# Moving work at both ends of a fused S5 + Mish-MLP kernel: a sum in the tail, two transposes and one layernorm in the head

## The chip, the cores and the metric

The kernel runs on one core of one Trainium2 chip. The metric is the device time of one execution in microseconds (us). Every execution quoted here is of the undisturbed ("fast") state, with a granted TensorE clock of 0.999 or 1.0. Engines are named as in the profile: PE (TensorE matmul), PEld (its weight loads), DVE (VectorE), ACT (ScalarE), POOL (GpSimd), SP (SyncE, here only a DMA queue).

## The reference, cut to what matters

```python
def reference(A_x, Lambda.., B.., C.., log_dt, Dskip, B_x, w1, b1, w2):   # S = 2048, D = 1024, F = 3584
    x  = A_x
    xn = _layernorm(x)
    # _A_ref: Bu = xn @ B_bar.T; h_t = Lam_bar * h_(t-1) + Bu_t; y = 2 Re(h @ C.T) + xn * Dskip
    # _B_ref: h = xn @ w1 + b1; act = h * tanh(softplus(h)); act @ w2
    return x + _A_ref(xn, ...) + _B_ref(xn, w1, b1, w2)
```

The 2048 tokens are worked in four blocks of 512. A block consists of: the 28 weight tiles of `w1` (PE, each evicted by DVE), the projection of the state inputs (PE, evicted by DVE into `mt`), the recurrence as scans (DVE), and the output sums of `w2` and `C` over eight units, one PSUM bank each (PE).

## The kernel before

The head of the program. Layernorm of the first four token tiles, transposes on PE, and small filler matmuls that keep PE busy while its clock rises:

```python
    keep_busy(44)                       # filler matmuls, 128x128
    ... transpose of the parameters
    keep_busy(12)
    for q in range(2):                  # tiles 0 and 1: statistics on DVE, root on ACT
        first_sums_v(q, 0); first_sums_v(q, 1); first_var_v(q); first_sqrt(q)
    first_apply(0)                      # DVE: xn of tile 0
    first_transpose(0)                  # PE: eight 128x128 transposes
    keep_busy(4)
    first_apply(1)
    first_transpose(1)
    keep_busy(4)
    first_copy(0, VE, 0, 4); first_copy(1, VE, 0, 4)      # PSUM -> xnT
    first_copy(0, AC, 4, NK); first_copy(1, AC, 4, NK)
    first_mean_a(3)                     # tile 3: sums on ACT, behind ACT's copies
    ... tile 2's statistics on DVE, tile 3's on ACT
    first_apply(2); first_apply(3)
    NSPLIT = 6
    for f in range(NSPLIT):             # first six weight tiles on tokens 0..255 only
        first_half(f, 0)                # eight 128x256 matmuls
        if f in (2, 4):
            q = 1 + f // 2              # tile 2 behind the third, tile 3 behind the fifth weight tile
            first_transpose(q)
            first_copy(q, VE)
```

Then small DVE operations give `thp`, and POOL starts its phases from it: eight times three operations (`px`, `py`, `ph`), 128x512 f32 in SBUF, with the loads of block 1's `x` issued by POOL in between:

```python
    def phases(j):
        pop(tensor_scalar(px, iot, thp[j], mult)); pop(tensor_scalar(py, px, +magic, -magic)); pop(tensor_tensor(xs, px, py, subtract))
    for j in range(NJ):
        phases(j)
        if j == 3:
            for q in range(NQ): load_x(PO, 1, q)
```

The tail of the last block:

```python
        for q in range(NQ):
            units = (2 * q, 2 * q + 1) if not (ends and q == NQ - 1) else (2 * q,)
            ... proj(j, ci, u, ...) for the last NJ - njt .. NJ
            finish(q, 0, len(units) * TB)                            # DVE: xx += ps, then store from ACT
        if ends:
            tmp, b_tmp = ct[0]
            vop(tensor_tensor(tmp, ps[:, 7, :], xx[:, i, 3, TB:D], add))      # first sum of unit 7
            for h in range(2):
                ... proj_quarter(...)                                # six 128x256 matmuls
                vop(tensor_tensor(xx[...], ps[:, h, 0:256], tmp[...], add))
                out_events["end", h] = AC.dma(...)                   # both stores issued by ACT
```

Of the kernel before, what the change touches and what calls it, by code (L numbers as in the profile page):

```python
# [5 lines left out]
ALU = mybir.AluOpType  # L6
# [150 lines left out]
def build_kernel(nc, A_x, A_Lambda_re, A_Lambda_im, A_B_re, A_B_im, A_C_re, A_C_im,  # L157
                 A_log_dt, A_Dskip, B_w1, B_b1, B_w2, out):
    bf16, f32, i32 = DT.bfloat16, DT.float32, DT.int32
    S, D = A_x.shape[1], A_x.shape[2]  # L160
    NP = A_Lambda_re.shape[0]
    F = B_w1.shape[1]
    TB = 512
    NB = S // TB
    NQ = TB // P
    NK = D // P
# [9 lines left out]
    VE = Queue(nc, "ve")  # L176
    AC = Queue(nc, "ac")
    PO = Queue(nc, "po")
    SP = Queue(nc, "sp")

    def sb(name, shape, dtype):
# [26 lines left out]
    xx = sb("xx", [P, 2, NQ, D], bf16)  # L208
    b_xx = [[Buf("xx%d_%d" % (i, q), parts=[Buf("xx%d_%d_%d" % (i, q, h)) for h in range(2)])
             for q in range(NQ)] for i in range(2)]  # L210
    s_xx = [[DmaSem(nc, "d_xx%d_%d" % (i, q)) for q in range(NQ)] for i in range(2)]
    xn = sb("xn", [P, NQ, D], bf16)
    b_xn = [Buf("xn%d" % q) for q in range(NQ)]
    mt = sb("mt", [P, 2, 2, TB], bf16)
    b_m = [Buf("m%d" % i) for i in range(2)]
    dsk = sb("dsk", [P, D], bf16)
# [5 lines left out]
    b_ident = Buf("ident")  # L222
# [142 lines left out]
        aop(lambda e: e.activation(rc(q, 1), mv[:, q, 1:2], AF.Sqrt, scale=scale, bias=kon[:, 2:3]),  # L365
            reads=[b_mv[q], b_kon], writes=[b_rs1[q]])

    def first_apply(q):
        y = rc(q, 1)
        vop(lambda e: e.reciprocal(y, y), reads=[b_rs1[q]], writes=[b_rs1[q]])  # L370
        vop(lambda e: e.tensor_scalar(xn[:, q, :], xx[:, 0, q, :], mv[:, q, 0:1], y,
                                      op0=ALU.subtract if q < 3 else ALU.add, op1=ALU.mult),
            reads=[b_xx[0][q], b_mv[q], b_rs1[q]], writes=[b_xn[q]])

    def bank_T(q, k):
        if q < 2 and k >= NK // 2:
# [3 lines left out]
    def first_transpose(q):  # L380
        for k in range(NK):
            bank = bank_T(q, k)
            PE.mm(lambda e, k=k, bank=bank: e.transpose(ps16(bank)[:, k * P:(k + 1) * P],  # L383
                                                        xn[:, q, k * P:(k + 1) * P], ident[:]),
                  reads=[b_xn[q], b_ident], writes=[b_ps[bank]],
                  first=k == 0 or bank != bank_T(q, k - 1), last=k == NK - 1 or bank != bank_T(q, k + 1))

    def first_copy(q, queue, k0=0, k1=NK):
        dst = xnT[:, k0:k1, q * P:(q + 1) * P]
        bank = bank_T(q, k0)  # L390
        srcp = ps16(bank).rearrange("p (k t) -> p k t", k=NK)[:, k0:k1, :]
        b_dst = b_xnT[q] if k1 - k0 == NK else b_xnT[q].parts[k0 // 4]
        if queue is AC:
            aop(lambda e: e.copy(dst, srcp), reads=[b_ps[bank]], writes=[b_dst])
        else:
            vop(lambda e: e.tensor_copy(dst, srcp), reads=[b_ps[bank]], writes=[b_dst])  # L396
# [63 lines left out]
    def keep_busy(n):  # L460
        for i in range(n):
            PE.mm(lambda e: e.matmul(ps[:, 3, 0:P], lhsT=ident[:], rhs=ident[:], start=True, stop=True),  # L462
                  reads=[b_ident], writes=[b_ps[3]], first=i == 0, last=i == n - 1)

    keep_busy(44)
    aop(lambda e: e.activation(rs[:, :, 3], kon[:, 2:3].to_broadcast([P, NQ]), AF.Sqrt), reads=[b_kon], writes=b_rs)
    PE.op(lambda e: e.transpose(ps16(2)[:, 0:NST], st[:, :], ident[0:NST, 0:NST]),  # L467
          reads=[b_st, b_ident], writes=[b_ps[2]])
# [5 lines left out]
        first_sqrt(q)  # L474
    first_apply(0)
    first_transpose(0)
    keep_busy(4)
    first_apply(1)
    first_transpose(1)
    keep_busy(4)  # L480
    first_copy(0, VE, 0, 4)
    first_copy(1, VE, 0, 4)
    first_copy(0, AC, 4, NK)
# [8 lines left out]
    first_sqrt(3)  # L492
    first_apply(2)
    first_apply(3)
    NSPLIT = 6

    def first_half(f, half):
        s, fi = f // 2, f % 2
        wt = ring[:, s, :].rearrange("p (k f) -> p k f", k=NK)
        ts = slice(half * 256, half * 256 + 256)  # L500
        for k in range(NK):
            PE.mm(lambda e, k=k: e.matmul(ps[:, f, ts], lhsT=wt[:, k, fi * P:(fi + 1) * P], rhs=xnT[:, k, ts],  # L502
                                          start=k == 0, stop=k == NK - 1),
                  reads=[b_ring[s]] + [b.parts[k // 4] for b in b_xnT[2 * half:2 * half + 2]], writes=[b_ps[f]],
                  first=half == 0 and k == 0, last=half == 1 and k == NK - 1)

    for f in range(NSPLIT):
        first_half(f, 0)
        if f in (2, 4):
            q = 1 + f // 2  # L510
            first_transpose(q)
            first_copy(q, VE)

    aop(lambda e: e.activation(c("dt"), ldt, AF.Exp), reads=[b_par], writes=[b_cs["dt"]])
    small("a", "dt", lre, ALU.mult)
# [198 lines left out]
    out_events = {}  # L714
    b_end = [Buf("end%d" % h) for h in range(2)]
    def tail(blk):
        first = [True] * 8

        def acc(u, lhsT, rhs, reads, last=False):
            st_ = first[u]  # L720
            first[u] = False
            PE.mm(lambda e: e.matmul(ps[:, u, :], lhsT=lhsT, rhs=rhs, start=st_, stop=last),  # L722
                  reads=reads, writes=[b_ps[u]], first=st_, last=last)

        def dense(f, s, units):
            wt = ring[:, s, :].rearrange("p (f d) -> p f d", f=2)
            for u in units:
                q, h = u // 2, u % 2
                acc(u, act[:, f, q * P:(q + 1) * P], wt[:, f % 2, h * TB:(h + 1) * TB], [b_actf[f], b_ring[s]])

        def proj(j, ci, u, last):
            q, h = u // 2, u % 2
            acc(u, hT[:, ci, j, q * P:(q + 1) * P], CT[:, ci, j, h * TB:(h + 1) * TB], [b_hT[ci][j], b_CT[j]], last)

        def proj_quarter(j, ci, bank, lo, st_, last):
            PE.mm(lambda e: e.matmul(ps[:, bank, 0:256], lhsT=hT[:, ci, j, 3 * P:4 * P], rhs=CT[:, ci, j, lo:lo + 256],
                                     start=st_, stop=last),
                  reads=[b_hT[ci][j], b_CT[j]], writes=[b_ps[bank]], first=st_, last=last)

        njt = 1 if blk == 0 else 3  # L740
        base = n_item[0]
        for f in range(6):
            dense(f, (base + f // 2) % NRING, (4, 5, 6, 7))
        for f in range(NF):
            dense(f, (base + f // 2) % NRING, (0, 1, 2, 3) if f < 6 else range(8))
            if f % 2 == 1:
                item_done()
            if blk + 1 < NB and f in (7, 9, 11, 13):
                transpose_dma((f - 7) // 2)
        for j in range(NJ - njt):  # L750
            for ci in range(2):
                for u in range(8):
                    proj(j, ci, u, blk == NB - 1 and u == 7 and j == NJ - njt - 1 and ci == 1)
        i = blk % 2

        def store(q, lo, hi, sem):
            r0 = blk * TB + q * P
            b_x = b_xx[i][q] if hi - lo > TB else b_xx[i][q].parts[lo // TB]
            out_events[i, q, lo] = AC.dma(lambda e: e.dma_start(out[0, r0:r0 + P, lo:hi], xx[:, i, q, lo:hi]),
                                          sem, reads=[b_x])  # L760

        def finish(q, lo, hi):
            bank, n = 2 * q + lo // TB, (hi - lo) // TB
            b_x = b_xx[i][q] if n > 1 else b_xx[i][q].parts[lo // TB]
            xr = xx[:, i, q, lo:hi]
            src = ps[:, bank:bank + n, :].rearrange("p a t -> p (a t)")
            vop(lambda e: e.tensor_tensor(xr, src, xr, op=ALU.add), reads=b_ps[bank:bank + n] + [b_x], writes=[b_x])  # L767
            store(q, lo, hi, s_out[i][q])

        ends = blk == NB - 1  # L770
        for q in range(NQ):
            units = (2 * q, 2 * q + 1) if not (ends and q == NQ - 1) else (2 * q,)
            for j in range(NJ - njt, NJ):
                for ci in range(2):
                    for u in units:
                        proj(j, ci, u, j == NJ - 1 and ci == 1)
            finish(q, 0, len(units) * TB)
        if ends:

            tmp, b_tmp = ct[0]  # L780
            b_x = b_xx[i][3].parts[1]
            vop(lambda e: e.tensor_tensor(tmp[:], ps[:, 7, :], xx[:, i, 3, TB:D], op=ALU.add),  # L782
                reads=[b_ps[7], b_x], writes=[b_tmp])
            for h in range(2):
                lo = TB + 256 * h
                for j in range(NJ - njt, NJ):
                    for ci in range(2):
                        proj_quarter(j, ci, h, lo, j == NJ - njt and ci == 0, j == NJ - 1 and ci == 1)
                vop(lambda e, h=h, lo=lo: e.tensor_tensor(  # L789
                    xx[:, i, 3, lo:lo + 256], ps[:, h, 0:256], tmp[:, 256 * h:256 * h + 256], op=ALU.add),  # L790
                    reads=[b_ps[h], b_tmp], writes=[b_end[h]])
                r0 = blk * TB + 3 * P
                out_events["end", h] = AC.dma(lambda e, lo=lo, r0=r0: e.dma_start(
                    out[0, r0:r0 + P, lo:lo + 256], xx[:, i, 3, lo:lo + 256]), DmaSem(nc, "d_end%d" % h), reads=[b_end[h]])
        if blk + 2 < NB:
            for q in range(NQ):
                load_x(PO, blk + 2, q)
# [81 lines left out]
```

## Time and profile before

The three runs before the prediction took 622.5, 623.05 and 625.32 us. The profiled execution took 621.96 us and spans 620.5.

| stretch of the profiled run | us | what it is |
|---|---|---|
| 0 to 8.69 | 8.7 | loads, layernorm of two tiles, fillers, transposes |
| 8.69 to 20.25 | 11.6 | six split weight tiles, transposes of tiles 2 and 3 |
| 20.25 to 616.56 | 596.3 | PE without a pause |
| 616.56 to 620.5 | 3.9 | last sums and stores |

The chain of waits of the kernel before, followed back from the last instruction (start in us, length in us, engine, tile, line):

```profile
8.69 2.78 PE ps L502 x24
...
14.21 6.20 PE ps L502 x56
20.41 37.99 PE ps L644 x176
58.40 27.63 PE ps L664 x128
86.03 75.97 PE ps L722 x352
...
616.58 0.69 DVE xx L767
617.27 0.61 DVE ct L782
...
617.98 0.76 DVE xx L789 x2
```

PE carries it nearly alone. L502 are the split tiles, L644 the full weight tiles, L664 the projection, L722 the output sums.

Two more lines of the same profile follow. The first is the table of busy times of 28 to 91 us (the columns are stretch, length, and busy us with instruction counts of PE, PEld, DVE, ACT and POOL, then clock, DMA share and GB/s):

```profile
28.00:91.00 63.00, 63.00 (x293) 28.58 (x292) 60.52 (x101) 59.02 (x44) 31.62 (x21) 1.00 1.05 232
```

The second is the only wait of PE or PEld between 20 and 110 us (engine, tile, line, whom it waited for: us in total, times, longest):

```profile
PEld ps L722 <- DVE mt L669: 0.3, 1, 0.3
```

A weight load waited for an `mt` eviction of DVE, at 91.46 us.

The tail in the timeline (start, length, engine, line; "q" is an engine's DMA issue):

```profile
615.29 1.99 DVE L767 TENSOR_TENSOR xx<-ps,xx 128x1024 bf16<-128x1024 f32 x2 [1.36 <-PE ps L722]
...
617.19 0.68 DVE L782 TENSOR_TENSOR ct<-ps,xx 128x512 f32<-128x512 f32 x1
617.98 0.76 DVE L789 TENSOR_TENSOR xx<-ps,ct 128x256 bf16<-128x256 f32 x2
618.43 0.82 ACTq L793 DMA_DIRECT2D out_dram<-xx  x2
```

PE's last matmul ends at 617.85. Behind it stand a sum that could have been made long before (L782), two quarter sums, and two stores issued one after the other.

### The profile page before, as it was taken

How to read it: one execution, taken by the hardware profiler on the slowest of the kernel's cores; microseconds unless marked ns; L12 is line 12 of the kernel's file. 1: busy time of each engine (PE TensorE's matmuls, PEld its weight loads, DVE VectorE, ACT ScalarE, POOL GpSimd, SP SyncE). 2: the span in 40 equal slices, each digit the busy share in tenths (PEclk: the TensorE clock that was granted, in tenths of full speed). 3: DMA queues.
4: the chain of work that ended last, by engine and by line, in shares of the span. 5: the costliest groups of instructions: out<-in, count | busy, mean ns of one | idle time of the engine just before them, and what ended most of it. 6: DMA issues, size and time to landing. Idle time of an engine off the chain costs nothing.

```text
span 620.5 us, 7405 instructions
## 1 busy us (share of the span) xinstructions
PE 616.3 (99%) x2967; PEld 288.1 (46%) x2967; DVE 466.3 (75%) x689; ACT 244.8 (39%) x158; POOL 49.9 (8%) x47
## 2 busy tenths in 40 slices
PE   8999999999999999999999999999999999999998
PEld 8544444444444444444444444444444444444443
DVE  6899999999467599998147659999624856999603
ACT  5679995440079940000009992000001999000000
POOL 1998000000100000000010000000000000000000
PEclk9999999999999999999999999999999999999999
DMA  9999967740464301773065420285204541033001
GB/s 262 239 274 270 223 142 205 202 136 0 161 178 141 132 1 40 217 185 103 17 191 165 140 99 1 98 209 167 70 35 137 168 137 67 1 135 104 1 0 69
DMA packets 124476, 79.41 MB, mean 128 GB/s; under 512 B 48922, under 2 KB 106906, under 8 KB 124442
## 3 DMA queue, kind: packets, MB, share of 16 engines
q1 hardware_dynamic: 120800, 71.58, 42.6%
q10 hardware_dynamic: 2682, 4.21, 1.9%
q0 software_dynamic: 960, 3.15, 1.7%
q8 instruction: 24, 0.39, 0.3%
q14 instruction: 10, 0.08, 0.0%
HBM read 63.19 MB, written 4.19 MB: 109 GB/s over the span
## 4 chain that ended last, share of the span: by engine, by line
PE 99%; DVE 0%; POOL 0%; issue 0%; DVEq 0%; POOLq 0%
PE ps L722 49%; PE ps L644 29%; PE ps L664 18%; PE ps L502 2%; PE ps L462 1%; PE ps L383 0%; DVE xx L789 0%; DVE xx L767 0%; DVE ct L782 0%; DVE xnT L396 0%; POOL ident L330 0%; POOL ident L329 0%; DVE par L486 0%; PE ps L467 0%; POOL kon L333 0%
## 5 line engine op out<-in xcount | busy, mean ns | idle before, releaser
L722 PE MATMUL ps<-ring,act 128*128 128x512 bf16 x896 | 194.0, 379 | 0.0
L644 PE MATMUL ps<-xnT,ring 128*128 128x512 bf16 x848 | 183.7, 379 | 0.0
L622 ACT ACTIVATE act<-hb 128x3584 bf16<-128x3584 bf16 x16 | 51.0, 3185 | 244.1 <-DVE hb L651 243.8
L722 PEld LDWEIGHTS ps<-ring,act 128*128 128x128 bf16 x896 | 87.6, 98 | 105.8 <-DVE mt L669 0.3
L644 PEld LDWEIGHTS ps<-xnT,ring 128*128 128x128 bf16 x848 | 83.0, 98 | 99.9
L651 DVE TENSOR_SCALAR hb<-ps,par 128x512 bf16<-128x512 f32 x112 | 82.7, 746 | 55.1 <-PE ps L644 53.6
L664 PE MATMUL ps<-xnT,BT 128*128 128x512 bf16 x512 | 111.2, 379 | 0.0
L722 PE MATMUL ps<-CT,hT 128*128 128x512 bf16 x506 | 109.9, 379 | 0.0
L669 DVE TENSOR_TENSOR mt<-ps,tab 128x1024 bf16<-128x1024 f32 x64 | 75.4, 1219 | 13.3 <-PE ps L664 11.7
L664 PEld LDWEIGHTS ps<-xnT,BT 128*128 128x128 bf16 x512 | 50.1, 98 | 60.4
L722 PEld LDWEIGHTS ps<-CT,hT 128*128 128x128 bf16 x506 | 49.5, 98 | 59.7
L767 DVE TENSOR_TENSOR xx<-ps,xx 128x1024 bf16<-128x1024 f32 (+1 forms) x16 | 18.8, 1190 | 69.5 <-PE ps L722 69.4
L687 DVE TENSOR_TENSOR_SCAN hT<-cs,qi,hT 128x512 bf16<-128x512 f32 x48 | 58.9, 1269 | 0.0
L624 ACT ACTIVATE act<-act 128x3584 bf16<-128x3584 bf16 x16 | 51.1, 3192 | 0.2
L623 ACT ACTIVATE act<-act 128x3584 bf16<-128x3584 bf16 x16 | 51.1, 3192 | 0.2
L692 DVE TENSOR_TENSOR mt<-hT,tab 128x1024 bf16<-128x1024 bf16 x64 | 41.4, 688 | 1.1
L629 DVE TENSOR_TENSOR act<-act,hb 128x3584 bf16<-128x3584 bf16 x16 | 32.3, 2018 | 1.3 <-ACT act L624 1.3
L287 POOL DMA_DIRECT2D xx<-in_A_x_dram x12 | 6.7, 560 | 253.0 <-DVE xx L767 248.7
L598 ACT ACTIVATE ct<-CT,cs 128x512 f32<-128x512 bf16 x16 | 11.5, 720 | 28.8 <-DVE CT L600 24.5
L623 ACT ACT_TABLE_LOAD x16 | 20.5, 1283 | 0.3
L624 ACT ACT_TABLE_LOAD x16 | 20.5, 1283 | 0.3
L687 DVE TENSOR_TENSOR_SCAN hT<-cs,hT 128x512 bf16<-128x512 f32 x16 | 18.7, 1208 | 0.0
(82 smaller groups left out, 281.3 us busy)
## 6 DMA issues: line engine op xcount, KB each, us to landing
ring<-in_B_w_dram SPq DMA_DIRECT2D x112, 512.0 KB, 3.8
out_dram<-xx ACTq DMA_DIRECT2D x15, 256.0 KB, 2.1
xx<-in_A_x_dram POOLq DMA_DIRECT2D x12, 256.0 KB, 4.6
xx<-in_A_x_dram SPq DMA_DIRECT2D x3, 256.0 KB, 5.0
xx<-in_A_x_dram SPq DMA_DIRECT2D x2, 128.0 KB, 2.1
dsk<-in_A_Dskip_dram SPq DMA_DIRECT2D x1, 256.0 KB, 6.7
xnT<-xn SPq DMA_TRANSPOSE x12, 4.5
BT<-in_A_B_re_dram SPq DMA_TRANSPOSE x8, 6.0
```

The lines of the kernel that those rows point to most:

```text
L622: aop(lambda e: e.activation(a, hs, AF.Exp), reads=[b_hb[g % 2]], writes=[b_act[g]])
L623: aop(lambda e: e.activation(a, a, AF.Ln, bias=1.0), reads=[b_act[g]], writes=[b_act[g]])
L624: aop(lambda e: e.activation(a, a, AF.Tanh), reads=[b_act[g]], writes=[b_act[g]])
L629: vop(lambda e: e.tensor_tensor(a, a, hs, op=ALU.mult), reads=[b_act[g], b_hb[g % 2]], writes=[b_act[g]])
L644: PE.mm(lambda e, k=k: e.matmul(ps[:, bank, :], lhsT=wt[:, k, fi * P:(fi + 1) * P], rhs=xnT[:, k, :], start=k == 0, stop=k == NK - 1), rea ...
L651: vop(lambda e: e.tensor_scalar(hb[:, hs, :], ps[:, bank, :], b1(f), None, op0=ALU.add), reads=[b_ps[bank], b_par], writes=[b_hbf[hs]])
L664: PE.mm(lambda e, j=j, ci=ci, k=k, bank=bank: e.matmul(ps[:, bank + ci, :], lhsT=BT[:, ci, j, k, :], rhs=xnT[:, k, :], start=k == 0, stop= ...
L669: vop(lambda e, s=s, u=u, j=j: e.tensor_tensor(mt[:, s, :, :], u, tab[:, s, j, :].unsqueeze(1).to_broadcast([P, 2, TB]), op=ALU.mult), rea ...
L687: vop(lambda e, ci=ci, init=init: e.tensor_tensor_scan(out=hT[:, ci, j, :], data0=cj("r", j).to_broadcast([P, TB]), data1=hT[:, ci, j, :], ...
L692: vop(lambda e, s=s: e.tensor_tensor(mt[:, s, :, :], hT[:, :, j, :], tab[:, s, j, :].unsqueeze(1).to_broadcast([P, 2, TB]), op=ALU.mult), ...
L722: PE.mm(lambda e: e.matmul(ps[:, u, :], lhsT=lhsT, rhs=rhs, start=st_, stop=last), reads=reads, writes=[b_ps[u]], first=st_, last=last)
L767: vop(lambda e: e.tensor_tensor(xr, src, xr, op=ALU.add), reads=b_ps[bank:bank + n] + [b_x], writes=[b_x])
```

## The change

The intent in the tail: make the first sum of the last unit early, while DVE is idle, and issue the two end stores from two queues. In the head: put the transposes of tiles 2 and 3 inside and behind the fourth weight tile, so that five split tiles are enough; apply tile 1's layernorm in halves, so that its transposes can start on the first half; and move the fillers to where PE would wait.

```diff
@@ -210,7 +210,7 @@
              for q in range(NQ)] for i in range(2)]
     s_xx = [[DmaSem(nc, "d_xx%d_%d" % (i, q)) for q in range(NQ)] for i in range(2)]
     xn = sb("xn", [P, NQ, D], bf16)
-    b_xn = [Buf("xn%d" % q) for q in range(NQ)]
+    b_xn = [Buf("xn%d" % q, parts=[Buf("xn%d_%d" % (q, h)) for h in range(2)]) for q in range(NQ)]
     mt = sb("mt", [P, 2, 2, TB], bf16)
     b_m = [Buf("m%d" % i) for i in range(2)]
     dsk = sb("dsk", [P, D], bf16)
@@ -365,12 +365,15 @@
         aop(lambda e: e.activation(rc(q, 1), mv[:, q, 1:2], AF.Sqrt, scale=scale, bias=kon[:, 2:3]),
             reads=[b_mv[q], b_kon], writes=[b_rs1[q]])
 
-    def first_apply(q):
+    def first_apply(q, pieces=1):
         y = rc(q, 1)
         vop(lambda e: e.reciprocal(y, y), reads=[b_rs1[q]], writes=[b_rs1[q]])
-        vop(lambda e: e.tensor_scalar(xn[:, q, :], xx[:, 0, q, :], mv[:, q, 0:1], y,
-                                      op0=ALU.subtract if q < 3 else ALU.add, op1=ALU.mult),
-            reads=[b_xx[0][q], b_mv[q], b_rs1[q]], writes=[b_xn[q]])
+        for h in range(pieces):
+            d = slice(h * D // pieces, (h + 1) * D // pieces)
+            b_x, b_o = (b_xx[0][q], b_xn[q]) if pieces == 1 else (b_xx[0][q].parts[h], b_xn[q].parts[h])
+            vop(lambda e, d=d: e.tensor_scalar(xn[:, q, d], xx[:, 0, q, d], mv[:, q, 0:1], y,
+                                               op0=ALU.subtract if q < 3 else ALU.add, op1=ALU.mult),
+                reads=[b_x, b_mv[q], b_rs1[q]], writes=[b_o])
 
     def bank_T(q, k):
         if q < 2 and k >= NK // 2:
@@ -382,7 +385,7 @@
             bank = bank_T(q, k)
             PE.mm(lambda e, k=k, bank=bank: e.transpose(ps16(bank)[:, k * P:(k + 1) * P],
                                                         xn[:, q, k * P:(k + 1) * P], ident[:]),
-                  reads=[b_xn[q], b_ident], writes=[b_ps[bank]],
+                  reads=[b_xn[q].parts[k // (NK // 2)], b_ident], writes=[b_ps[bank]],
                   first=k == 0 or bank != bank_T(q, k - 1), last=k == NK - 1 or bank != bank_T(q, k + 1))
 
     def first_copy(q, queue, k0=0, k1=NK):
@@ -462,7 +465,7 @@
             PE.mm(lambda e: e.matmul(ps[:, 3, 0:P], lhsT=ident[:], rhs=ident[:], start=True, stop=True),
                   reads=[b_ident], writes=[b_ps[3]], first=i == 0, last=i == n - 1)
 
-    keep_busy(44)
+    keep_busy(48)
     aop(lambda e: e.activation(rs[:, :, 3], kon[:, 2:3].to_broadcast([P, NQ]), AF.Sqrt), reads=[b_kon], writes=b_rs)
     PE.op(lambda e: e.transpose(ps16(2)[:, 0:NST], st[:, :], ident[0:NST, 0:NST]),
           reads=[b_st, b_ident], writes=[b_ps[2]])
@@ -474,10 +477,9 @@
         first_sqrt(q)
     first_apply(0)
     first_transpose(0)
-    keep_busy(4)
-    first_apply(1)
+    first_apply(1, 2)
     first_transpose(1)
-    keep_busy(4)
+    keep_busy(6)
     first_copy(0, VE, 0, 4)
     first_copy(1, VE, 0, 4)
     first_copy(0, AC, 4, NK)
@@ -492,24 +494,27 @@
     first_sqrt(3)
     first_apply(2)
     first_apply(3)
-    NSPLIT = 6
-
-    def first_half(f, half):
+    NSPLIT = 5
+
+    def first_half(f, half, k0=0, k1=NK):
         s, fi = f // 2, f % 2
         wt = ring[:, s, :].rearrange("p (k f) -> p k f", k=NK)
         ts = slice(half * 256, half * 256 + 256)
-        for k in range(NK):
+        for k in range(k0, k1):
             PE.mm(lambda e, k=k: e.matmul(ps[:, f, ts], lhsT=wt[:, k, fi * P:(fi + 1) * P], rhs=xnT[:, k, ts],
                                           start=k == 0, stop=k == NK - 1),
                   reads=[b_ring[s]] + [b.parts[k // 4] for b in b_xnT[2 * half:2 * half + 2]], writes=[b_ps[f]],
                   first=half == 0 and k == 0, last=half == 1 and k == NK - 1)
 
     for f in range(NSPLIT):
-        first_half(f, 0)
-        if f in (2, 4):
-            q = 1 + f // 2
-            first_transpose(q)
-            first_copy(q, VE)
+        first_half(f, 0, 0, NK // 2)
+        if f == 3:
+            first_transpose(2)
+            first_copy(2, VE)
+        first_half(f, 0, NK // 2, NK)
+        if f == 3:
+            first_transpose(3)
+            first_copy(3, VE)
 
     aop(lambda e: e.activation(c("dt"), ldt, AF.Exp), reads=[b_par], writes=[b_cs["dt"]])
     small("a", "dt", lre, ALU.mult)
@@ -768,6 +773,11 @@
             store(q, lo, hi, s_out[i][q])
 
         ends = blk == NB - 1
+        if ends:
+            tmp, b_tmp = ct[0]
+            b_x7 = b_xx[i][3].parts[1]
+            vop(lambda e: e.tensor_tensor(tmp[:], ps[:, 7, :], xx[:, i, 3, TB:D], op=ALU.add),
+                reads=[b_ps[7], b_x7], writes=[b_tmp])
         for q in range(NQ):
             units = (2 * q, 2 * q + 1) if not (ends and q == NQ - 1) else (2 * q,)
             for j in range(NJ - njt, NJ):
@@ -777,10 +787,6 @@
             finish(q, 0, len(units) * TB)
         if ends:
 
-            tmp, b_tmp = ct[0]
-            b_x = b_xx[i][3].parts[1]
-            vop(lambda e: e.tensor_tensor(tmp[:], ps[:, 7, :], xx[:, i, 3, TB:D], op=ALU.add),
-                reads=[b_ps[7], b_x], writes=[b_tmp])
             for h in range(2):
                 lo = TB + 256 * h
                 for j in range(NJ - njt, NJ):
@@ -790,7 +796,7 @@
                     xx[:, i, 3, lo:lo + 256], ps[:, h, 0:256], tmp[:, 256 * h:256 * h + 256], op=ALU.add),
                     reads=[b_ps[h], b_tmp], writes=[b_end[h]])
                 r0 = blk * TB + 3 * P
-                out_events["end", h] = AC.dma(lambda e, lo=lo, r0=r0: e.dma_start(
+                out_events["end", h] = (SP, AC)[h].dma(lambda e, lo=lo, r0=r0: e.dma_start(
                     out[0, r0:r0 + P, lo:lo + 256], xx[:, i, 3, lo:lo + 256]), DmaSem(nc, "d_end%d" % h), reads=[b_end[h]])
         if blk + 2 < NB:
             for q in range(NQ):
```

## The prediction

> **What bounds the kernel now.** PE. On the page PE is busy 616.3 us of the 620.5 us span; in the chain of waits it holds 99%, and from 8.69 us (first real matmul) to 616.56 us it runs through four blocks with no wait. The change touches only the two ends.
>
> **Tail (timeline, 607 to 620.5).** Last PE result about 617.85. DVE before: unit 6's sum 616.58 (0.69), the first sum of unit 7 617.19 (0.68), then two quarter sums 617.98 and 618.33 (0.42 each); both stores are issued by ACT one after the other (618.43, 618.85; 0.41 each), the last lands 1.7 us later and ends the span. Bank 7's first sum is complete about 607.5, and DVE idles until 610.11, so moving it there is free. Then: first quarter sum 617.23 (when its matmuls are done), its store on SP; second quarter sum 617.88 to 618.30, store at 618.35, landing about 620.0. Saves 0.5 us, all critical.
>
> **Head (timeline, 6 to 21).** Matmul work hardly changes (128x256 matmuls start every 109 ns, 128x512 every 216: one split tile less saves 0.02 us). What counts is stalls; before there are two of 0.09 us (tile 2's transpose waits for xn at 11.40; the second token half waits for the copy of tile 3 at 14.99).
> - Four more fillers delay tile 0's transpose: it starts at 7.02, behind the twelve fillers, though its xn ended at 6.85. Estimate +0.2 us (44 fillers took 4.8 us, about 107 ns each; the twelve after 6.3 us 57 ns each). The Trainium skill ("TensorE: Matmul & The Clock Gate", Part 1) says the activity window is free-running, so this varies by run; this trace shows one such change only.
> - Removing the four fillers between the transposes gives that back to tile 1: it starts at 7.69 as before. The halves of its layernorm hide nothing then (xn ended at 7.50). First real matmul still about 8.7.
> - ACT's two copies follow tile 0's transpose, so they end 0.2 later (9.15 for 8.93), and with them tile 3's whole ACT chain (mean 1.15, square 1.13, root 0.29, then DVE 0.16 and 0.55): xn of tile 3 is ready about 13.1 for 12.88.
> - PE now asks for tile 3's transpose after four tiles and one transpose, about 8.7+0.07+3.95 = 12.7, where before it asked at 13.60 and had 0.7 us of slack. New stall about 0.45 us, plus some 0.1 for the copy of tile 3 before the second half, and 0.07 in tile 0 for the ACT copies.
>
> Head, less tile 2's stall: about +0.4 us. Nothing later absorbs it, since PE never waits later.
>
> **Sum.** +0.4 - 0.5 = about -0.1 us: no visible change. Predicted 622.8 us, 8 in 10 between 621.8 and 624.0. Faster by over 2%: 0.005; within 2%: 0.99; slower by over 2%: 0.005.
>
> **What would show it.** Right: in the timeline the first-sum DVE instruction stands near 607.6 (relative to PE's end), the last store is issued 0.5 us after PE's last matmul ends instead of 1.0; PE idles 0.3 to 0.5 us before tile 3's transposes, released by DVE's xn; tile 0's transposes start 0.2 later, tile 1's at the same time. Wrong: no idle there, or the first real matmul before 8.5.
>
> **What would make it wrong.** The clock rising at another moment (moves the head by up to 0.4); a weight slot landing later than PE asks; a slower store from SP; a faster ACT chain; or run-to-run noise larger than the effect, which I expect.

## More of the kernel before

In block 0 DVE does more than evict weight tiles. Between the evictions stand coefficients, the skip product `x += xn * dsk` (lines with `mt<-xn,dsk` and `xx<-xx,mt`), and the layernorm of block 1:

```python
            if f in (7, 8, 9, 10):      coefficients(f - 7)
            if f in (9, 11, 12, 13):    ln_skip(0, ...)
            if f in (14, 16, 18, 20):   ln_stats_only(1, (f - 14) // 2)
            if f == 22:                 ln_rsqrt()
            if f in (23, 24, 25, 26):   ln_scale(1, f - 23)
        ...
        project_in(blk)        # per j: 16 matmuls, then DVE: two 'mt<-ps,tab', two 'hT<-mt'
```

The output sums of a block begin with the four units whose banks come free first. The other four need the last `mt` evictions of the projection:

```python
        for f in range(6):
            dense(f, ..., (4, 5, 6, 7))                              # 24 matmuls
        for f in range(NF):
            dense(f, ..., (0, 1, 2, 3) if f < 6 else range(8))       # waits for mt of the last two j
```

## The result, and the profile after

The changed kernel: 623.32 us median of 6 runs (622.52 to 623.98). The kernel before in the same comparison: 622.58 (621.94 to 625.32). The ratio of the fast runs is 1.0005, 95% interval 0.9985 to 1.0024: no difference at 2%. Ratios in this text are the mean time of one kernel's fast runs over that of the other's of the same rounds, so they are not quite the ratio of the quoted medians. Here one run of 625.32 lifts the mean of before, so the means differ by only 0.3 us where the medians differ by 0.7. By both the changed kernel is the slower one, but the interval does not exclude a tie.

The profiled execution took 623.57 us and spans 622.1, which is 1.6 us more than that of before. Its chain of waits:

```profile
11.60 1.48 PE ps L504 x12
...
19.74 39.71 PE ps L649 x184
59.45 27.63 PE ps L669 x128
87.08 4.12 PE ps L727 x19
...
91.22 2.37 DVE mt L674 x2
...
93.63 70.54 PE ps L727 x326
...
620.06 0.42 DVE xx L795
```

The first sums of units 4 to 7 (L727, L722 before) begin 1.05 us later than before (87.08 for 86.03). Then there is something new: at 91.22 the chain leaves PE for two `mt` evictions of DVE and returns to PE at 93.63. PE's own wait in that place (the view of waits), and below it the busy times of 90 to 100 us (columns as above, PE first):

```profile
PE ps L727 <- DVE mt L674: 0.9, 1, 0.9
```

```profile
90.00:100.00 10.00, 9.06 (x43) 3.95 (x42) 9.73 (x13) 8.06 (x6) 0.00 (x0) 1.00 0.55 150
```

The tail, with lines that answer to those of before:

```profile
609.69 0.69 DVE L779 TENSOR_TENSOR ct<-ps,xx 128x512 f32<-128x512 f32 x1 [23.45 <-PE ps L727]
...
619.41 0.42 DVE L795 TENSOR_TENSOR xx<-ps,ct 128x256 bf16<-128x256 f32 x1
619.86 0.36 SPq L799 DMA_DIRECT2D out_dram<-xx  x1
620.06 0.42 DVE L795 TENSOR_TENSOR xx<-ps,ct 128x256 bf16<-128x256 f32 x1 [0.23 <-PE ps L741]
620.52 0.34 ACTq L799 DMA_DIRECT2D out_dram<-xx  x1
```

The first sum (L779) is out of the way. From the end of PE's last matmul to the end of the span it is 2.12 us (620.02 to 622.14), where it was 2.70 (617.85 to 620.55).

The difference of the two profiled runs, put together from the traces:

| place | before, us | after, us | adds |
|---|---|---|---|
| seventh weight tile begins (end of the head) | 20.25 | 21.30 | +1.05 |
| block 1's first weight tile begins | 161.84 | 164.01 | +1.12 more |
| PE's last matmul ends | 617.85 | 620.02 | 0 more |
| end of the span | 620.55 | 622.14 | -0.58 |

(After has five split tiles, so its seventh tile is the second of full width: 19.58 us plus eight matmuls of 216 ns.)

In the head of this run, PE waited for a load at the third weight tile (idle before it in brackets), and tile 3's transposes then followed without a wait:

```profile
11.60 1.48 PE L504 MATMUL ps<-xnT,ring 128*128 128x256 bf16 x12 [0.51 <-DMA ring<-in_B_w_dram]
12.92 0.61 PE L386 MATMUL ps<-ident,xn 128*128 128x128 bf16 x8
13.36 0.60 PE L504 MATMUL ps<-xnT,ring 128*128 128x256 bf16 x4
13.80 0.61 PE L386 MATMUL ps<-ident,xn 128*128 128x128 bf16 x8
```

Two questions follow. Is the 1.1 us near 93 us an effect of the change or bad luck? And what does each part of the change do alone?

### The profile page after: what moved, and what is told of

Read it like the earlier page. It is cut to its first block, busy times and chain, and to the rows that moved or that the text cites. A ratio compares the mean times of both kernels' runs of the same rounds, so it can differ in the third digit from the quotient of the medians.

```text
span 622.1 us, 7394 instructions
## 1 busy us (share of the span) xinstructions
PE 617.1 (99%) x2961; PEld 287.8 (46%) x2961; DVE 467.2 (75%) x690; ACT 244.6 (39%) x158; POOL 50.9 (8%) x47
## 4 chain that ended last, share of the span: by engine, by line
PE 97%; DMA 1%; DVE 0%; SPq 0%; issue 0%
PE ps L727 48%; PE ps L649 30%; PE ps L669 18%; DMA ring<-in_B_w_dram 1%; PE ps L504 1%; DVE mt L674 0%; SPq L287 0%; PE ps L741 0%; PE ps L386 0%; SPq L291 0%; SPq L318 0%; DVE xx L795 0%
## 5 line engine op out<-in xcount | busy, mean ns | idle before, releaser
L727 PE MATMUL ps<-ring,act 128*128 128x512 bf16 x896 | 194.2, 379 | 0.9 <-DVE mt L674 0.9
L727 PEld LDWEIGHTS ps<-ring,act 128*128 128x128 bf16 x896 | 87.6, 98 | 106.9 <-DVE mt L674 1.4
L727 PE MATMUL ps<-CT,hT 128*128 128x512 bf16 x506 | 109.9, 379 | 0.0
L727 PEld LDWEIGHTS ps<-CT,hT 128*128 128x128 bf16 x506 | 49.5, 98 | 59.7
```

Source lines behind the costliest of these rows:

```text
L727: PE.mm(lambda e: e.matmul(ps[:, u, :], lhsT=lhsT, rhs=rhs, start=st_, stop=last), reads=reads, writes=[b_ps[u]], first=st_, last=last)
```

## The experiments

Twelve kernels ran, in three lots; each lot ran on one chip and shares its runs of the kernel before. Lots one and three were on the same chip, lot two on another. In lot one the kernel before shows two groups: six runs of 621.9 to 622.4 and five of 623.9 to 624.6. In lot three eight lie below 623 and three at 623.3 to 624.4. In lot two all nine lie between 621.93 and 622.47. All of these count as fast.

One measure recurs: the **DVE chain**, from the eviction of the tenth weight tile (the last one or nearly the last for which DVE still waits for PE) to the end of the last `mt` eviction of block 0. Before it is 64.05 us (27.36 to 91.41), after 65.16 us (28.41 to 93.57).

### tail_only: the tail part alone

```diff
+        if ends: ... vop(tmp = ps[7] + xx)          # ahead of the q loop, as in the change
-            vop(tmp = ps[7] + xx)                   # in the end part
-                out_events["end", h] = AC.dma(
+                out_events["end", h] = (SP, AC)[h].dma(
```

> The kernel before with the tail part alone (first sum of unit 7 ahead of the last evacuations, first end store issued by SP). Theory: all of it lies on the critical path; from PE's last matmul end to the end of the span it takes 0.5 to 0.6 us less, and the time falls by 0.5 us. Rival (the tail's gain is given back by the store issued on SP or by contention of the last stores): time within 0.2 us of before.

Measured: 622.28 us median (621.34 to 624.03), before 622.41; ratio 0.9988 (0.9969 to 1.0007). From the end of PE's last matmul to the end of the span: 2.12 us. The three quickest runs (621.34, 621.66, 621.80) lie 0.5 us in the mean below before's quickest three (621.92, 622.12, 622.16), so no part of the gain appears to be given back. The profile fell into a run of the slower group (624.03 us) and so shows one thing that makes a run slow. DVE's waits between 28 and 110 us, then PE's:

```profile
DVE stats L405 <- DMA xx<-in_A_x_dram: 2.8, 1, 2.8
...
PE ps L722 <- DVE mt L669: 1.2, 1, 1.2
PE ps L664 <- DVE hb L651: 0.8, 1, 0.8
```

Block 1's statistics stand in DVE's queue before evictions of block 0. Here the load of `x` that they read landed 9.6 us after its issue; in the profile of before it was 4.7. DVE waited 2.8 us, and 2.0 us of that reached PE.

### head_only: the change without its tail

```diff
   (the diff above, less its last three hunks)
```

> The change without its tail part. Theory as predicted: the head costs 0.4 us or more, so this kernel is 0.4 to 1.5 us slower than before; the full-width matmuls of the seventh tile start 0.4 to 1.0 us later than 20.25 us. Rival (the profiled run of the change was only unlucky with its loads and vector locks): within 0.2 us of before.

Measured: 623.77 us median (623.32 to 624.15); before 622.41 us; ratio 1.0007, which is an even result only because before's mean holds its slow group. Against the mean of before's quick group (622.19 us) the mean (623.74) is 1.55 us more. The seventh tile began at 21.59 us, after a wait of 0.81 us for the load of the second weight slot, and PE waited 0.9 us for `mt` at 93.65, as in the changed kernel. The DVE chain took 65.11 us. So the wait near 93 us belongs to the head part, twice out of two.

### before_dve_more: 1.6 us more DVE work in block 0

```diff
             if f in (14, 16, 18, 20):
                 ln_stats_only(1, (f - 14) // 2)
+                if f == 14:
+                    ln_stats_only(1, 0)             # once more, same result
```

> The kernel before with one tile's layernorm statistics of block 1 computed twice in block 0 (same result, 1.6 us more DVE work after the ninth tile). Theory of two level paths (in block 0 DVE's chain ends level with PE's, at the first output matmuls of the first four units near 91 us): the time rises by 1.2 to 1.7 us and PE shows a wait for the mt evictions of that size. Rival (PE alone sets the time and DVE has slack in block 0): no change, within 0.2 us.

Measured: 624.13 us median (623.77 to 626.34); ratio 1.002 (1.0002 to 1.0039). Without its slowest run, which was the profiled one, the mean is 624.11, that is 1.9 us over before's quick group. So work added to an engine that is not on the chain of before seems to cost its full length or more, as it must if PE and DVE are level in block 0. This run alone does not prove it: 623.8 to 624.5 us is also where before's slow group lies (five of its eleven runs, against all six here), and 1.9 us is more than the 1.6 added. In the profiled run a load of `x` was late as well (DVE waited 4.3 us), so its PE waits, 3.3 us in sum, are of both causes and are not used here.

### after_relief: 1.8 us less DVE work in block 0 of the changed kernel

```diff
-            if f in (23, 24, 25, 26):
-                ln_scale(1, f - 23)
...
         project_in(blk)
+        if blk == 0:
+            for q in range(NQ):
+                ln_scale(1, q)
```

> The changed kernel with the four layernorm applications of block 1 (about 0.45 us of DVE each) moved from inside block 0's tile loop to behind its projection, so DVE's chain up to 91 us is 1.8 us shorter. Theory of two level paths: the wait of 0.9 us that PE shows near 91 us in the changed kernel goes, and the time falls by 0.5 to 1.2 us. Rival (PE alone): no change, within 0.2 us, or slower if the scans then come late.

Measured: 621.86 us median, all six runs within 621.5 to 622.01; ratio 0.9978 (0.9962 to 0.9993). The wait near 93 us is gone. Against the changed kernel (623.32, and 623.07 in the third lot) it is 1.2 to 1.5 us faster, a little more than expected. That the rest is other lateness of DVE, which this kernel also absorbs, is likely but not shown. Against the mean of before's quick group (622.19 us) the mean (621.83) is 0.36 us less, so most of the ratio's gain comes from before's slow group.

### before_relief, tail_relief, head_relief: the parts without the DVE chain

The same move of `ln_scale`, applied to the kernel before, to tail_only and to head_only. These ran on the chip where before shows one group (622.24 us median).

> The kernel before with the four layernorm applications of block 1 moved behind block 0's projection (as in after_relief). Its timed runs so far fall in two groups, about 622.2 and 624.2 us. Theory of two level paths: the slow group is block 0's DVE chain coming late to PE; with 1.8 us taken off that chain the slow group goes, all runs lie within 0.5 us of each other near 622.2 us, and PE shows no wait between 20 and 110 us. Rival (the two groups come from the loads in the head or from the chip): both groups stay.

Measured: 622.26 us median (621.9 to 622.83), no PE wait between 20 and 110 us; ratio 1.0003. The question whether the slow group goes could not be answered here, since the kernel before did not show it on this chip. The runs lie 0.9 us apart, more than expected. DVE still waited 1.0 us for a load of `x` in the profile, and PE did not feel it.

> before_relief with the tail part of the change. Theory: 0.5 to 0.6 us less than before_relief, runs within 0.5 us of each other, about 621.6 us: faster than both kernels. Rival (the tail's gain is not real): equal to before_relief.

Measured: 621.76 us median (621.42 to 622.35); means 621.80 against 622.35 of before_relief, 0.55 us less. That agrees with the tail's 0.58 us of the traces, and more closely than five runs each, 0.9 us apart, can show; the traces carry the claim (from PE's last matmul to the end of the span 2.69 us in before_relief, 2.12 here).

> before_relief with the head parts of the change, so the head's own cost is read without the DVE chain behind it. Theory as predicted: 0.3 to 0.6 us more than before_relief, with a PE wait of 0.4 to 0.8 us for the xn of tile 3 before its transposes. Rival (the head costs nothing by itself, only through the DVE chain): within 0.15 us of before_relief.

Measured: 622.22 us median (622.11 to 622.88); mean 622.39, equal to before_relief. The seventh tile began at 20.41 us for 20.32. So in this pair of profiles, with loads in time and DVE out of the way, **the head part costs 0.1 us, not the 0.4 that I had predicted**. The means alone, of runs 0.8 to 0.9 us apart, could not tell the two. The predicted wait for tile 3 is there. PE in this run's timeline, then DVE:

```profile
12.16 0.60 PE L504 MATMUL ps<-xnT,ring 128*128 128x256 bf16 x4
12.90 0.62 PE L386 MATMUL ps<-ident,xn 128*128 128x128 bf16 x8
...
12.29 0.55 DVE L374 TENSOR_SCALAR xn<-xx,mv,rs 128x1024 bf16<-128x1024 bf16 x1
```

Four matmuls from 12.16 would have let the transposes start at 12.60 (four times 109 ns); they started at 12.90, when xn of tile 3 was done at 12.84. That is 0.3 us lost. It is largely paid for: here tile 1's transposes began at 7.58 us for 7.76 in before_relief, so the first real matmul came 0.1 us earlier (8.66 for 8.76), and the small wait for tile 2 is gone. The four more fillers did not delay tile 0 in this run (7.06 for 7.08): the last one ended at 6.67, and xn of tile 0 was done only at 7.00. Part of that is luck, since the fillers' spacing fell from 107 to 56 ns at 4.6 us here and at 5.6 us in before_relief. In the first profile of the changed kernel it fell at 7.4 us, and the fillers held tile 0 back.

### before_less_pool: fewer POOL operations (wrong result)

```diff
-    for j in range(NJ):
+    for j in range(2):
         phases(j)
-        if j == 3: ...                               # loads of block 1's x now behind the second
...
-        src, b_src = ph_slot(j)
+        src, b_src = ph_slot(j % 2)                  # tables of six tiles are wrong
```

> The kernel before with two of POOL's eight phase groups (the tables of the other six tiles are then wrong, on purpose; the work of DVE, ACT and PE is the same). Theory: the lateness of DVE's chain is made by waits of DVE's two-input SBUF operations on POOL operations; without these the skip operations (mean 0.86 and 1.11 us in the kernel before, 0.69 undisturbed) all take 0.69 us, DVE's chain is 3 to 5 us shorter, PE does not wait near 91 us, and all runs lie near 622.2 us. Rival (POOL does not matter): the operations stay as long and the two groups of times stay.

Measured: 621.85 us median (621.68 to 622.51). (The outputs nevertheless passed the comparison with the reference.) The DVE chain took 61.06 us, 3.0 us less than before. (Against before it had gained 4.2 us by the end of block 1's statistics; then DVE waited 2.1 us in all for PE's projection and gave part of that back.) The skip product in the groups of 28 to 62 us (count, busy us, mean ns, idle before), in the kernel before:

```profile
L436 DVE TENSOR_TENSOR xx<-xx,mt 128x1024 bf16<-128x1024 bf16 x4 | 4.5, 1114 | 0.1
L434 DVE TENSOR_TENSOR mt<-xn,dsk 128x1024 bf16<-128x1024 bf16 x4 | 3.4, 857 | 0.0
```

and with POOL idle:

```profile
L436 DVE TENSOR_TENSOR xx<-xx,mt 128x1024 bf16<-128x1024 bf16 x4 | 2.8, 692 | 0.1
L434 DVE TENSOR_TENSOR mt<-xn,dsk 128x1024 bf16<-128x1024 bf16 x4 | 2.7, 682 | 0.0
```

So POOL's operations do stretch DVE's. The Trainium skill says so: "SBUF — State Buffer", section "SBUF: two separate sides", describes one port pair that DVE and GpSimd share as an exclusive lock, taken for a whole instruction, and DVE operations with two SBUF inputs or in a two-port mode need it. These traces fit such a lock: the two-input skip products vary from 0.68 to 1.71 us, while evictions that read PSUM keep to a mean of 0.74 us. They agree on "a whole instruction" only for one of POOL's three operations, as shown below. How such a wait looks, in the kernel before, DVE and then POOL:

```profile
35.20 1.38 DVE L434 TENSOR_TENSOR mt<-xn,dsk 128x1024 bf16<-128x1024 bf16 x1
36.61 1.06 DVE L436 TENSOR_TENSOR xx<-xx,mt 128x1024 bf16<-128x1024 bf16 x1
...
34.76 1.27 POOL L528 TENSOR_TENSOR ph_h<-px,py 128x512 f32<-128x512 f32 x1
```

and in the changed kernel:

```profile
34.85 1.71 DVE L437 TENSOR_TENSOR mt<-xn,dsk 128x1024 bf16<-128x1024 bf16 x1
36.59 1.06 DVE L439 TENSOR_TENSOR xx<-xx,mt 128x1024 bf16<-128x1024 bf16 x1
...
34.74 1.27 POOL L533 TENSOR_TENSOR ph_h<-px,py 128x512 f32<-128x512 f32 x1
```

In both, a product of DVE (the third token tile's before, the second's after) starts while the POOL operation (34.76 to 36.03, and 34.74 to 36.01) runs, and ends about 0.55 us after it. In the changed kernel it starts 0.1 us after POOL's begin instead of 0.44, and so loses 0.33 us more. The change adds no DVE work here. It moves DVE against POOL, and the losses fall otherwise.

That pair is an example of the wait, not the place where the time goes. Over the whole DVE chain, each operation's time less the quickest of its kind in all profiles, the skip products lose 2.4 us before and 2.5 after. The small coefficient operations (`cs`, 128x8) lose 0.7 and 1.5: most of the difference is one of them, which began together with POOL's `ph` and took 1.28 us instead of 0.17. Before, then after with its POOL operation:

```profile
28.29 0.37 DVE L452 TENSOR_TENSOR cs<-cs 128x8 f32<-128x8 f32 x2
...
29.35 1.48 DVE L455 TENSOR_TENSOR cs<-cs 128x8 f32<-128x8 f32 x2
29.54 1.27 POOL L533 TENSOR_TENSOR ph_h<-px,py 128x512 f32<-128x512 f32 x1
```

The kind of POOL operation matters too. Over the chains of all fourteen profiles, 32 two-input DVE operations (skip products, coefficients, layernorm) began during a `ph`, which itself has two SBUF inputs. All 32 lost 0.70 to 1.11 us, and none ended before the `ph` did. During `px` or `py`, with one SBUF input, 229 began: 29, all in the first 0.62 us of the POOL operation, lost 0.32 to 0.43 us and the others next to nothing, and 206 ended before POOL's operation. (The profile's times of POOL are rough.) An example from the kernel before:

```profile
38.97 1.06 DVE L436 TENSOR_TENSOR xx<-xx,mt 128x1024 bf16<-128x1024 bf16 x1
...
38.36 2.02 POOL L524 TENSOR_SCALAR px<-iot,cs 128x512 f32<-128x512 f32 x1
```

That gave a sharper theory. In every profile with the head part POOL's first phase starts 12.7 us before the tenth eviction; in every one without it, 11.9 us (before: 15.48 to 27.36; after: 15.69 to 28.41). The DVE chain is 65.1 us with the first distance and 64.05 with the second, apart from what a kernel took out or a late load put in. The 0.85 us is one split weight tile (eight matmuls of 109 ns, 0.87 us): tile 3's copy, on which `thp` and with it POOL's start depend through DVE's order, comes after one weight tile less. Lot three tests this.

### after_again: the changed kernel on the chip of lot three

> The changed kernel once more, on the chip of the next three. Theory of the vector lock: as in every profile with the head part so far, POOL's first phase operation starts 12.7 us before DVE evicts the tenth weight tile (11.9 without the head part), the DVE chain from there to the last mt eviction takes 65.1 us (64.05), and PE waits about 1 us near 93 us. Time 623.0 to 623.8. Rival (the wait was bad luck of two runs): no wait near 93 us and about 622.2.

Measured: 623.07 us median (622.96 to 623.63); before 622.52; ratio 1.0008 (0.9996 to 1.002). Distance 12.73 us (15.83 to 28.56), chain 65.10 us, PE wait:

```profile
PE ps L727 <- DVE mt L674: 0.9, 1, 0.9
```

All as expected, and on top of it a wait of 1.26 us for the second weight slot in the head.

### after_pool_later: POOL gets one operation more

```diff
     turns()
+    pop(tensor_scalar(px[:, 0:256], iot[:, 0:256], thp[0], mult))     # written over by the next one
     for j in range(NJ):
         phases(j)
```

> The changed kernel with one more POOL operation (half a phase product, written over by the next, same result) ahead of the phases, so that POOL's phases start about 0.85 us later, where they stood against DVE before the change. Theory of the vector lock: adding this work makes the kernel faster. The chain from the tenth eviction to the last mt eviction falls from 65.1 to about 64.1 us, PE's wait near 93 us falls from about 1.0 to 0.1 us or less, the time falls by 0.8 to 1.0 us against after_again. Rival (the longer DVE chain has another cause, and the phases' place does not matter): time and chain stay as in after_again.

Measured: 622.56 us median (621.9 to 623.7); mean 622.66 against 623.20 of after_again: 0.54 us less, where 0.8 to 1.0 was expected. The trace shows the mechanism whole. The added operation puts the first full phase at 16.75 us instead of 15.71, 11.7 us before the tenth eviction at 28.43. The chain falls to 64.07 us. PE's wait near 93 us is gone, and what is left is the weight-load wait of the kernel before:

```profile
PEld ps L729 <- DVE mt L676: 0.3, 1, 0.3
```

From the seventh tile's begin to block 1's first tile it takes 141.39 us, where after_again takes 142.42 and before 141.59. The timed runs spread over 1.8 us, from 621.9 to 623.7. I did not profile the slow ones; that late loads fill the rest of the gap is not shown.

### no_placement: fillers, halves and tail, but the transposes where they were

```diff
-    NSPLIT = 5
+    NSPLIT = 6
     ... transposes of tiles 2 and 3 behind the third and fifth weight tile, as before
```

> The change without its middle part: six split tiles and the transposes of tiles 2 and 3 behind the third and fifth tile as before; fillers, halves and tail as in the change. Theory: it is the one tile (0.87 us) fewer before tile 3's transpose that moves POOL's start against DVE, so here the distance is 11.9 us again, the chain 64.05 us, no PE wait near 91 us; the time is that of tail_only in its quick runs, 621.3 to 621.9, 0.5 us below before and 1.3 to 1.6 below after_again. Rival (fillers or halves move it): distance 12.7, PE waits, 623.

Measured: 622.12 us median (621.62 to 624.19); ratio 0.9996 (0.9981 to 1.0011). Distance 11.88 us (15.72 to 27.60), chain 64.02 us, no PE wait near 91 us. It is the placement that moves POOL; neither fillers nor halves do. Three of six runs lie at 621.6 to 621.9, where all were expected; the others (622.36, 622.90, 624.19) show that this kernel is as open to late loads as before.

### no_placement_relief: the same with the DVE chain shortened

```diff
   no_placement, with ln_scale(1, q) behind project_in as in after_relief
```

> no_placement with the four layernorm applications moved behind the projection, so that neither the lock nor a late load of block 1's x (waits of 2.8 and 4.3 us in the slow runs of tail_only and before_dve_more) reaches PE. Theory: fastest of all, 621.3 to 621.8 and all runs within 0.6 us. Rival: no better than no_placement, where the loads come in time.

Measured: 621.81 us median (621.6 to 622.33); ratio 0.9985 (0.9972 to 0.9998). It is the fastest of its lot, 1.3 us under after_again in both mean and median, although in the profile PE waited 0.60 us for the second weight slot. Its runs lie 0.7 us apart. Of the twelve, this one and after_relief (0.9978) are faster than before by more than their intervals. In both cases before's mean holds its slow runs; against its runs under 623 us the gain is 0.5 us here and 0.36 there, no more than the tail's.

## Why the prediction was right or wrong

The range held: 623.32 us lies in 621.8 to 624.0, no visible change was forecast and none is visible at 2%. It held because it was 2.2 us wide, not because the account was complete: the sum behind it was wrong in two terms that do not cancel, and the forecast change of -0.1 us was +0.7 us in the medians.

- **Tail, right.** Predicted 0.5 us saved, all critical. Measured 0.58 us between PE's last matmul and the end (2.70 to 2.12 us in the traces), and 0.55 us in the means of tail_relief and before_relief. The store from SP shows no loss in the traces.
- **Head by itself, direction right, size off.** Predicted +0.4 us. In head_relief, where loads come in time, it is +0.1. The new wait for tile 3 exists where no late weight load stands before it (0.3 us, for the predicted 0.45, in head_relief, after_relief and after_pool_later). In the changed kernel's first profile PE waited for a load instead and there was no idle time before tile 3's transposes, which the prediction had named as a sign that it was wrong. The terms mis-sized are the filler delay (0 us there, not 0.2, with the early clock that is noted above) and tile 1's transposes, which I had put "at 7.69 as before" and which came 0.18 us earlier. In the changed kernel's own profiled run the clock rose late, near 7.4 us, so tile 0's transposes started at 7.74, and a load made PE wait 0.5 us. The head then cost 1.05 us. The prediction named both risks.
- **"Nothing later absorbs it, since PE never waits later": this step failed.** Nothing absorbed it, true, but something was added. I had read "PE has no wait" as "DVE has time in hand". It had none: the weight load's wait of 0.3 us in the profile of before, and DVE's 60.5 busy of 63 us, said so. The change puts POOL's start 0.85 us earlier against DVE, DVE's chain up to 93 us then takes 1.1 us longer, most of it in operations that run beside POOL's, and as the two engines were level, about 1 us of it reaches PE. This is shown from both sides: the wait goes with 1.8 us less DVE work (after_relief), with POOL put back later (after_pool_later), and without the placement (no_placement).
- **Noise.** "Run-to-run noise larger than the effect" was right, but it is not featureless. A slow run of tail_only has a late load of block 1's `x` in DVE's queue. That the slow group of the kernel before is of the same kind is likely, since it shares that code, but no slow run of it was profiled. The timed runs speak for it: on the chip of lots one and three 8 of before's 22 runs lie over 623 us, and none of the 11 runs of after_relief and no_placement_relief, whose DVE chain is 1.8 us shorter.

Put together for the chip of lots one and three: against before's quick runs the change is worth -0.58 us in the tail, +0.1 us or more in the head, and about +1.0 us through DVE. That is +0.5 us or somewhat more; the measured difference is 623.20 (after_again) less 622.41 (before's runs under 623 us in the same lot), 0.8 us. The 0.3 us between them is not explained; later loads in the head (below) are the nearest candidate.

What stays open: in the head, PE waited 0.5 to 1.3 us for the second weight slot in four of the eight profiles with the new fillers (after, head_only, after_again, no_placement_relief), and at most 0.12 us in the six with the old ones. The loads are issued in the same order in all, and the one waited for is issued at 3.8 us in thirteen of the fourteen (4.0 in after_again); it landed at 10.2 to 10.7 us with the old fillers and at 9.7 to 11.7 with the new. Whether this is chance is not settled.

## What to carry to other kernels

An engine that never waits may be level with another; before costing a change at one end, look for the shortest wait on the long engine's row, even one of its weight loads only, and for a second engine that is busy nearly throughout up to that point (here 60.5 of 63 us). A shift of 0.85 us between DVE and POOL cost more here (about 1.0 us) than the tail saved (0.58), so where both work on SBUF and DVE is level with PE, give DVE's chain some slack first. In the changed kernel, moving 1.8 us of DVE work behind the meeting point took 1.2 to 1.5 us off. In the kernel before, on the chip where it showed no slow group, it took nothing off (622.26 for 622.24 us).

## What the Trainium skill lacked or had wrong

- "SBUF — State Buffer" has the lock of the shared port and says that the order of issue decides who waits. It gives no size for a chain of many operations: with the same DVE work after the tenth tile, a shift of 0.85 us changed the chain from 64.05 to 65.1 us in each profile, and one more POOL operation brought it back to 64.07.
- The same page says that the first to start holds the pair for the whole instruction and the other fully blocks, also for a two-input DVE operation against any GpSimd operation that reads SBUF. Here that fits POOL's two-input `ph` (32 of 32 waited for its end), but not its one-input `px` and `py`: 200 of 229 two-input DVE operations begun during them lost nothing to speak of, and the other 29 lost at most 0.43 us.
- "TensorE: Matmul & The Clock Gate", Part 1, gives the transition as around 4 us of activity, plus or minus 0.5 us from run to run. In these traces the fillers' spacing fell from 107 to 56 ns between 4.26 us (no_placement_relief) and 7.41 us (the changed kernel), that is 2.8 to 6.0 us after the first filler at 1.42. A spread of 3.1 us is far wider than plus or minus 0.5; it is nearer to the free-running window of about 3.4 us that the page also states, though the earliest rise came before one such window had passed.
- "Perfetto Trace Analysis", section "Identifying Dependency Chains", says to look at the semaphores waited on. It lacks the case of two level chains: here a wait of 0.3 us on the weight-load row, with no idle PE at all, was the only wait of PE's rows in block 0 of the profile of before that showed it.
- No page read for this case gives the spread of a load's landing under other traffic. The same 256 KB loads of `x`, issued by POOL near 36 us, landed after 4.7 us in the profile of before and after 11.1 us in that of before_dve_more.
